# Filler matmuls in a two-layer transformer block: lower levels of estimated TensorE occupancy

## The chip, the cores and the metric

The kernel runs on one core of a Trainium2 chip. A core has five engines with queues of their own: TensorE (PE, matrix products into the PSUM memory), VectorE (DVE), ScalarE (ACT), GpSimd (POOL) and SyncE (SP, which here issues DMAs). They meet through semaphores only. The metric is the time of one execution in microseconds (us), as the device measures it. A change counts by the median of several runs. Beside the runs there is one profiled execution, from which all rows of the profile come.

## The reference

Two layers, each an attention block and a gated feed-forward block (FFN), both with a residual sum and a layer norm without weights. The same weights serve both layers.

```python
def _A_ref(x, wqkv, wo):              # x: 1 x 2048 x 512, 32 heads of 16
    qkv = (x @ wqkv).reshape(B, S, 3, H, Dh)   # then q, k, v by head
    scores = einsum("bhqd,bhkd->bhqk", q, k) * Dh ** -0.5
    p = softmax(scores)
    o = einsum("bhqk,bhkd->bhqd", p, v)
    return o.reshape(B, S, D) @ wo
def _B_ref(x, w_gate, w_up, w_down):  # 512 -> 1792 -> 512
    return (gelu(x @ w_gate) * (x @ w_up)) @ w_down

x = A_x
x = x + _A_ref(layernorm(x), wqkv, wo)
x = x + _B_ref(layernorm(x), w_gate, w_up, w_down)
...   # both lines once more
```

Inputs are bfloat16. A head has only 16 dimensions, so a score matmul fills few rows of the array, while every one of the 2048 x 2048 scores of 32 heads must be read out of PSUM.

## The kernel before

**The two passes over the scores.** The softmax needs the largest score of each row of queries. The kernel computes the scores twice. Pass 1 (line 1165, matmuls `PS<-KT,QT`) puts queries on partitions: a tile is 128 queries by 512 keys of one head, and DVE takes the maximum along the keys (line 1180). Usually two tiles lie in neighbouring banks of PSUM and one DVE instruction of 1024 columns takes both (a pair); where only one bank is free, one instruction takes one tile (a single). The maxima of a unit (four heads, up to 512 queries) are collected in PM, reduced and transposed on DVE (lines 684, 686) and moved by SP into a spare row of the queries QT (line 701). The keys KT hold ones in that row, so pass 2 (line 1062, `PS<-QT,KT`, keys on partitions) yields scores with the maximum already taken off. ACT takes the exponential of one or two tiles (line 1039) into SCR, and PE multiplies these by the values VP (line 1085), with a column of ones that sums the weights. A unit's sums are read by ACT (line 714) and divided on POOL (lines 720, 725). In a few places two tiles of pass 1 are folded: ACT writes the positive part of a difference (line 1019) and DVE adds and reduces in one custom instruction with a read of its result (line 1175).

Both passes use 32 rows of the array per matmul, and up to four such matmuls, on different rows, run at once. PSUM has eight banks: pass 1 has banks 0 to 3, pass 2 mostly 3 to 6, and bank 7 holds the sums of the values.

**Everything else** goes in between as chains of small steps: layer norm and transposes (line 576), projections of Q, K and V, the output projection and the FFN (all matmuls of line 494). Their results are read out by DVE or ACT, whichever the rule `pick` names by how far pass 1 leads pass 2. The second layer takes its queries in blocks of 512, 512, 512, 256 and 256; the first in four of 512. At the end DVE has no more reductions to do, ACT finishes the exponentials, and the last output projection and FFN follow.

**The planner.** The order of all instructions is made when the kernel is built. A loop (the `while True` behind `warm_emit`) keeps an estimated clock for each engine, `clk`. At each step it knows the estimated time `now` on PE and a list `act` of PE work, each with its columns at 1/2400 us, at a quarter for a matmul of 32 rows. From them it has the estimated occupancy of PE over the last 3.413 us:

```python
            load = sum(c for _, _, c in act) / 3.413
```

The loop then records the next piece of PE work with the instruction that reads its result: a pair or single of pass 1, a tile or two of pass 2, both, a piece of a chain, or a filler. A filler (`warm_emit`, line 1198) multiplies a zero matrix ZER with 240 columns of the value weights WV into a part of a bank that nobody reads, so it changes no result. It is a matmul of 128 rows and 240 columns.

The occupancy enters in two places. The slack that may be spent to record both passes together is 0.1 us where it is under the level WARM, else 0.15 us (line 1283):

```python
                if G <= min(max(S1, T1), max(S2, T2)) + (SPC if load < WARM else SPLIT):
```

And fillers (`want` is WARM, `must` is WARML; BOOST is 0):

```python
            cool = load < want and now > 12 and warm_bank(now) is not None
            if G is not None and now >= G - 0.02 and not (cool and load < must):
                ...
            if cool and (G is None or now + 0.12 <= lim or load < must):
                warm_emit(warm_bank(now))
```

Under the upper level a filler is recorded where the planner sees a hole of 0.12 us ahead of the next pair. Under the lower level it is recorded even where a pair is due. Since the order is fixed when the kernel is built, a filler that is recorded is executed wherever it stands. On the chip each engine works through its own list and waits on semaphores where it must.

## Time and profile before

| | |
|---|---|
| time, median of 3 runs (lowest to highest) | 2621.01 us (2617.53 to 2625.14) |
| the profiled execution: time, span | 2617.2 us, 2615.4 us |
| mean granted clock of TensorE | 0.999 |
| matmuls on PE, fillers among them | 30171, 2715 |
| maxima on DVE (line 1180): pairs, singles | 1464, 1024 |
| exponentials on ACT (line 1039): pairs, singles | 1550, 996 |

How to read it: the page gives busy time of each engine, and in it PE means matmuls and PEld the loading of weights, which overlaps them. A matmul's record reaches to the modelled end of its pipeline, so PE that is shown busy is not at its peak. Groups are by line, engine, operation and shape, with count, busy time, mean ns of one, and the idle time of the engine just before them with what ended it. The chain is followed back from the last instruction. A view of stretches gives busy time for each engine in each stretch and the clock that was granted to TensorE there, where 1.00 is full speed.

### The profile page before, as it was taken

To read this page: it belongs to the slowest core of one execution; us is meant where nothing else is said; L and a number is where in the kernel's file an instruction comes from. 1 tells how busy PE (TensorE), PEld (TensorE's weight loads), DVE (VectorE), ACT (ScalarE), POOL (GpSimd) and SP (SyncE) were. 2 spreads that over 40 slices of the span, in tenths; PEclk is the share of its full clock that TensorE was granted. 3 is DMA by queue.
4 is the path that set the end of the run, shared out by engine and by line. 5 is a ranking of instruction groups with operands and counts; after the bars stand their busy time and mean duration, and the time that the engine had idled before them with its cause. 6 is when DMAs were issued, how large, how long until landed. Compare 5 with 4: busy or idle time off the path is not lost.

```text
span 2615.4 us, 67983 instructions
## 1 busy us (share of the span) xinstructions
PE 2504.4 (96%) x30171; PEld 1186.5 (45%) x30171; DVE 2480.6 (95%) x2965; ACT 2341.4 (90%) x3172; POOL 540.8 (21%) x521
## 2 busy tenths in 40 slices
PE   7999999999999999999999999999999999999998
PEld 2444443444434444344423555544444445444555
DVE  7999999999999999999999999999999999999991
ACT  8799998999989998999952999979998899989996
POOL 3011022221222212222132111111112311232201
PEclk9999999999999999999999999999999999999999
DMA  3110000000000000000000000000000000000000
GB/s 101 34 56 8 4 4 2 4 4 4 4 3 3 4 4 3 8 4 12 9 8 9 2 4 4 4 4 6 8 6 4 6 6 3 4 4 11 4 6 5
DMA packets 27125, 25.03 MB, mean 10 GB/s; under 512 B 9168, under 2 KB 25808, under 8 KB 26832
## 3 DMA queue, kind: packets, MB, share of 16 engines
q1 hardware_dynamic: 26832, 20.69, 2.8%
q8 instruction: 236, 3.87, 0.6%
q14 instruction: 57, 0.47, 0.1%
HBM read 9.70 MB, written 2.10 MB: 5 GB/s over the span
## 4 chain that ended last, share of the span: by engine, by line
PE 51%; DVE 30%; ACT 18%; issue 1%; POOL 0%; POOLq 0%; ACTq 0%
DVE PM L1180 28%; ACT SCR L1039 16%; PE PS L1165 16%; PE PS L494 12%; PE PS L1085 11%; PE PS L1062 6%; PE PS L1198 5%; DVE SCR L1175 1%; PE PS L576 1%; PE PS L1012 0%; ACT AO L738 0%; DVE ST L521 0%; ACT SCR L1019 0%; ACT L1039 0%; DVE HT L820 0%
## 5 line engine op out<-in xcount | busy, mean ns | idle before, releaser
L1180 DVE TENSOR_REDUCE PM<-PS 128x2 f32<-128x1024 f32 (+1 forms) x2488 | 2327.9, 997 | 59.2 <-PE PS L1062 30.2
L1039 ACT ACTIVATE SCR<-PS 128x1024 bf16<-128x1024 f32 (+1 forms) x2546 | 2037.6, 878 | 87.4 <-PE PS L1062 44.1
L1062 PE MATMUL PS<-QT,KT 32*128 32x512 bf16 (+1 forms) x4608 | 988.0, 360 | 32.8 <-ACT SCR L1039 29.3
L1165 PE MATMUL PS<-KT,QT 32*128 32x512 bf16 x4024 | 974.0, 385 | 38.5 <-DVE PM L1180 21.9
L1085 PE MATMUL PS<-VP,SCR 128*128 128x51 bf16 (+1 forms) x16384 | 804.5, 188 | 6.3 <-ACT SCR L1039 3.7
L1085 PEld LDWEIGHTS PS<-VP,SCR 128*128 128x128 bf16 x16384 | 566.5, 96 | 491.0 <-issue 445.3
L1165 PEld LDWEIGHTS PS<-KT,QT 32*128 32x128 bf16 x4024 | 234.3, 91 | 517.2 <-DVE PM L1180 300.6
L1198 PE MATMUL PS<-WV,ZER 128*128 128x240 bf16 x2715 | 457.9, 266 | 5.6 <-ACT SCR L1039 4.9
L720 POOL TENSOR_TENSOR RL<-ACCS,CM 128x16 f32<-128x16 f32 (+1 forms) x64 | 175.9, 2749 | 1296.5 <-ACT ACCS L714 1296.5
L1062 PEld LDWEIGHTS PS<-QT,KT 32*128 32x128 bf16 x4608 | 244.1, 91 | 142.3 <-ACT SCR L1039 114.6
L1198 PEld LDWEIGHTS PS<-WV,ZER 128*128 128x128 bf16 x2715 | 207.5, 96 | 69.3 <-issue 49.7
L828 POOL TENSOR_TENSOR HT<-HT,AO 128x512 bf16<-128x512 bf16 (+1 forms) x105 | 111.5, 1062 | 312.7 <-ACT AO L826 312.6
L810 ACT ACTIVATE HT<-PS 128x512 bf16<-128x512 f32 (+1 forms) x126 | 69.0, 549 | 78.9 <-PE PS L494 78.0
L494 PE MATMUL PS<-WD,HT 128*128 128x512 bf16 x448 | 131.0, 382 | 1.5 <-POOL HT L828 1.4
L494 PE MATMUL PS<-XNT,WU 128*128 128x512 bf16 (+1 forms) x504 | 129.4, 358 | 1.7 <-DVE PM L1180 0.6
L494 PE MATMUL PS<-XNT,WG 128*128 128x512 bf16 (+1 forms) x504 | 121.4, 361 | 0.0
L740 POOL TENSOR_TENSOR X<-X,AO 128x512 f32<-128x512 f32 x43 | 54.4, 1267 | 216.2 <-ACT AO L738 216.2
L865 POOL TENSOR_TENSOR KD<-KT 128x512 bf16<-128x512 bf16 x71 | 81.7, 1152 | 47.1 <-PE PS L1012 47.1
L826 ACT ACTIVATE AO<-PS 128x512 f32<-128x512 f32 (+1 forms) x105 | 59.2, 564 | 12.0 <-PE PS L494 10.8
L494 PEld LDWEIGHTS PS<-XNT,WG 128*128 128x128 bf16 x504 | 38.9, 98 | 47.6 <-issue 28.5
L725 POOL TENSOR_TENSOR ATT<-ACCS,RL 128x256 bf16<-128x256 f32 (+1 forms) x72 | 41.1, 571 | 90.3 <-DVE RL L718 85.3
L494 PEld LDWEIGHTS PS<-XNT,WU 128*128 128x128 bf16 x504 | 34.0, 97 | 34.8 <-issue 22.4
(78 smaller groups left out, 801.0 us busy)
## 6 DMA issues: line engine op xcount, KB each, us to landing
KT<-SG SPq DMA_DIRECT2D x64, 64.0 KB
QT<-SG SPq DMA_DIRECT2D x56, 64.0 KB
QT<-MT SPq DMA_DIRECT2D x224, 1.0 KB
out_dram<-AO SPq DMA_DIRECT2D x16, 128.0 KB, 1.7
WG<-in_B_w_gate_dram SPq DMA_DIRECT2D x4, 448.0 KB, 5.1
WU<-in_B_w_up_dram SPq DMA_DIRECT2D x4, 448.0 KB, 3.9
WD<-in_B_w_down_dram SPq DMA_DIRECT2D x4, 384.0 KB, 4.5
SCR<-in_A_x_dram SPq DMA_DIRECT2D x2, 512.0 KB, 5.2
```

The costliest lines, as they stand in the source:

```text
L494: ins = e.matmul(out_ap, lhsT=l, rhs=r_, start=(i == 0), stop=(i == n - 1))
L720: emit("pool", lambda e: e.tensor_tensor(RL[:, s, 0:4 * nq], lsum, CM1[:, 0:4 * nq], op=ALU.pow), r=[("ACCS", s), ("CM1",)], w=[("RL", s)] ...
L810: emit("act", lambda e, bg=bg, ft=ft: e.activation(HT[:, ft, 0:n], bank(bg)[:, 0:n], ACTF.Gelu_apprx_tanh), r=[BK[bg]], w=[("HT", ft)], du ...
L826: emit("act", lambda e, bu=bu, o=o: e.activation(AO[:, o, 0:n], bank(bu)[:, 0:n], ACTF.Copy), r=[BK[bu]], w=[("AO", o)], dur=0.055 + n / 1 ...
L828: emit("pool", lambda e, ft=ft, o=o: e.tensor_tensor(HT[:, ft, 0:n], HT[:, ft, 0:n], AO[:, o, 0:n], op=ALU.mult), r=[("AO", o), ("HT", ft) ...
L865: emit("pool", lambda e: e.tensor_tensor(KD[:, s, :], KT[:, g, ka * 512:(ka + 1) * 512], KT[:, g, kb * 512:(kb + 1) * 512], op=ALU.subtrac ...
L1039: emit("act", lambda e: e.activation(dst, src, ACTF.Exp, scale=DH ** -0.5), r=[BK[bk + i] for i in range(cnt)], w=[("PT", i) for i in slot ...
L1062: ins = e.matmul(bank(bk)[:, i * n:(i + 1) * n], lhsT=KT[32 * j:32 * j + 32, g, kt * 128:(kt + 1) * 128], rhs=QT[32 * j:32 * j + 32, s, 0: ...
L1085: ins = e.matmul(acc, lhsT=PT[:, slot, i * n + qt * 128:i * n + (qt + 1) * 128], rhs=AP(VP, (kt * H + 4 * g + j) * 17, [[NTT * H * 17, 128 ...
L1165: ins = e.matmul(bank(b), lhsT=QT[32 * j:32 * j + 32, s, qt * 128:(qt + 1) * 128], rhs=KT[32 * j:32 * j + 32, g, kb * 512:(kb + 1) * 512], ...
L1180: emit("dve", lambda e: e.tensor_reduce(po, PS[:, bs[0]:bs[0] + cnt, :], axis=AX.X, op=ALU.max), r=bks, w=[("PM", sm) + h[1:] for h in hs] ...
L1198: return e.matmul(PS[:, b, NACC:512], lhsT=ZER[:, :], rhs=WV[:, 0, 0:512 - NACC], start=(b != 7), stop=(b != 7), skip_group_check=True)
```

## The change

Two default values of `_build` change: the upper level of estimated occupancy, WARM, from 0.55 to 0.46, and the lower one, WARML, from 0.42 to 0.34. Since the planner decides every step by what came before, the recorded order changes from the first few microseconds on, on every engine. The computation is the same.

```diff
 def _build(nc, x_in, wqkv, wo, wg, wu, wd, out, layer_blocks=((512, 512, 512, 512), (512, 512, 512, 256, 256)),
-           ..., PVC=47, WARM=0.55, WARML=0.42, NPV=10, BOOST=0.0, ...):
+           ..., PVC=47, WARM=0.46, WARML=0.34, NPV=10, BOOST=0.0, ...):
```

More of the change, by code (lines that the diff above doesn't have):

```diff
@@ L174, in _build @@
 def _build(nc, x_in, wqkv, wo, wg, wu, wd, out, layer_blocks=((512, 512, 512, 512), (512, 512, 512, 256, 256)),
-           n_ahead=6, n_pre=6, S1C=0.45, S2C=0.42, OV=0.3, PD=70, FDUE=20, LIM=-0.05, NT=1, AHD=2.0, DUEM=-4, FDL2=-8, OPD=-6, ft_tok=512, n_pt=8, n_qt=8, SPLIT=0.15, SPC=0.1, PVC=47, WARM=0.55, WARML=0.42, NPV=10, BOOST=0.0, LAG=62, LAGT=75, GP=2, SING=0, DUE=0, END=360, LAGE=10, FD=280, FDL=-10, QD=32, KD_=24, VD=20, FL=8, FMAX=6, NKD=2, FLOOK=2, FX=0.1):
+           n_ahead=6, n_pre=6, S1C=0.45, S2C=0.42, OV=0.3, PD=70, FDUE=20, LIM=-0.05, NT=1, AHD=2.0, DUEM=-4, FDL2=-8, OPD=-6, ft_tok=512, n_pt=8, n_qt=8, SPLIT=0.15, SPC=0.1, PVC=47, WARM=0.46, WARML=0.34, NPV=10, BOOST=0.0, LAG=62, LAGT=75, GP=2, SING=0, DUE=0, END=360, LAGE=10, FD=280, FDL=-10, QD=32, KD_=24, VD=20, FL=8, FMAX=6, NKD=2, FLOOK=2, FX=0.1):
     S = x_in.shape[1]
```

## The prediction

> **What bounds the kernel now.** I read the page first: the busy line, then the chain that ended last, then the fillers' own group.

> ```profile
> PE 2504.4 (96%) x30171; PEld 1186.5 (45%) x30171; DVE 2480.6 (95%) x2965; ACT 2341.4 (90%) x3172; POOL 540.8 (21%) x521
> ...
> PE 51%; DVE 30%; ACT 18%; issue 1%; POOL 0%; POOLq 0%; ACTq 0%
> ...
> L1198 PE MATMUL PS<-WV,ZER 128*128 128x240 bf16 x2715 | 457.9, 266 | 5.6 <-ACT SCR L1039 4.9
> ```

> Three engines are over 90% busy. PE's 96% says least, because matmuls overlap in the record and 2715 of PE's 30171 instructions are fillers. So I looked at each stage (stretch, its length, then busy time of PE, PEld, DVE, ACT, POOL, the granted clock of TensorE, and DMA):

> ```profile
> 75.00:700.00 625.00, 593.99 (x7523) 287.59 (x7523) 615.50 (x686) 591.29 (x816) 116.67 (x105) 1.00 0.04 12
> 700.00:1300.00 600.00, 581.06 (x6920) 266.00 (x6917) 590.38 (x669) 555.83 (x790) 136.75 (x117) 1.00 0.02 5
> 1300.00:1450.00 150.00, 145.60 (x836) 49.16 (x833) 140.68 (x211) 70.87 (x104) 43.79 (x53) 1.00 0.03 8
> 1450.00:2000.00 550.00, 532.64 (x7008) 263.82 (x7007) 538.05 (x659) 520.93 (x626) 79.43 (x56) 1.00 0.02 5
> 2000.00:2550.00 550.00, 535.86 (x6926) 260.76 (x6926) 527.01 (x640) 507.55 (x681) 129.91 (x125) 1.00 0.02 5
> 2550.00:2616.00 66.00, 55.54 (x648) 35.76 (x646) 11.54 (x25) 40.24 (x62) 9.91 (x16) 0.97 0.02 5
> ```

> DVE is the bound of layer 0: idle only 9.5 us of 625 and 9.6 of 600. In layer 1 DVE idles 12 and 23 us of 550, and in several 25 us slices there (1475 to 1500, 1575 to 1600, 1875 to 1900) ACT is busy for all 25.00 us, so the two take turns. From 75 to 2550 us DVE idles 63 us in all. That is the whole prize a freer PE can win in these stretches. Of it, DVE waits for PE (total us, times, longest):

> ```profile
> DVE PM L1180 <- PE PS L1062: 30.2, 113, 0.7
> DVE PM L1180 <- PE PS L1165: 10.3, 43, 0.6
> DVE SCR L1175 <- PE PS L1165: 2.1, 8, 0.7
> ```

> 42.6 us. (L1062 stands there because score matmuls of both passes sit in one group on PE.) Going through DVE's waits on matmuls one by one in the trace, 89 of them, 16.1 us, have a filler as PE's last work before the group that DVE waited for.

> The clock matters as much. Four windows of 3.41 us, a thin one in the middle of layer 1 and three at the end:

> ```profile
> 1559.17:1562.59 3.42, 2.89 (x43) 1.41 (x39) 3.03 (x6) 3.42 (x5) 1.41 (x1) 1.00 0.00 0
> 2583.17:2586.58 3.41, 3.17 (x26) 2.33 (x24) 1.90 (x4) 0.60 (x1) 1.27 (x1) 1.00 0.00 0
> 2586.58:2590.00 3.42, 0.40 (x4) 0.23 (x4) 0.42 (x2) 0.13 (x1) 2.59 (x5) 1.00 0.00 0
> 2590.00:2593.41 3.41, 3.22 (x18) 2.50 (x19) 0.42 (x1) 2.13 (x3) 0.13 (x1) 0.50 0.00 0
> ```

> After the window in which PE was busy 0.40 us, the granted clock is 0.50 for one window and then whole again. It is the only drop after the start. I cut the trace at that phase into windows and weighed streamed columns as the kernel's estimate does (a 32-row matmul at a quarter). Over 716 windows from 88 to 2532 us the weighted share is 0.554 in the mean, 0.388 at least (the thin window shown), and 0.063 in the window ahead of the drop. All this trace says of the level that drops the clock is that it lies between 0.063 and 0.388.

> **The change part by part.** Prices are busy time over count from these rows, since successive instructions overlap a little: DVE pair 1734.2/1464 = 1.185 us, DVE single 690.5/1024 = 0.674, ACT pair 1536.5/1550 = 0.991, ACT single 599.7/996 = 0.602.

> ```profile
> L1180 DVE TENSOR_REDUCE PM<-PS 128x2 f32<-128x1024 f32 x1464 | 1734.2, 1218 | 48.0 <-PE PS L1062 26.3 <-PE PS L1165 14.0
> L1039 ACT ACTIVATE SCR<-PS 128x1024 bf16<-128x1024 f32 x1550 | 1536.5, 1054 | 74.7 <-PE PS L1062 37.7 <-PE PS L1165 9.6
> ...
> L1180 DVE TENSOR_REDUCE PM<-PS 128x1 f32<-128x512 f32 x1024 | 690.5, 682 | 11.3 <-PE PS L1062 3.8 <-PE PS L1165 2.5 <-PE PS L1012 0.5
> L1039 ACT ACTIVATE SCR<-PS 128x512 bf16<-128x512 f32 x996 | 599.7, 603 | 12.7 <-PE PS L1062 6.4
> ```

> The planner's lists of both programs can be counted without running them.

> *Fillers.* 1552 in place of 2715, 1163 fewer. Fillers in a run start 0.103 us apart (a run of four takes 0.57 us, a single one 0.26), so PE is given back 1163 x 0.103 = 120 us. Most of it lay in holes while PE waited for a bank and is worth nothing; the cover is DVE's own queue. What counts is the part ahead of due work. Counted where they are recorded, 167 fillers of before displaced a pair that was due (estimate below the lower level); 63 do in the changed program: 104 x 0.103 = 10.7 us. The other way: 43% of the 16.1 us of DVE waits right behind a filler is 6.9 us. Bounds: nothing, if DVE then waits for its bank or for its own queue; 43% of all 63 us of DVE's idle time = 27 us. I take 9, between the two counts.

> *Split tiles.* The same estimate picks between two slacks for pairing the passes (line 1283), and everything behind is reordered. Layer 0 on DVE: 7 pairs fewer, 18 singles more, 4 folded tiles (0.725 us with its read) fewer: -8.3 + 12.1 - 2.9 = +0.9 us, in full on the path. Layer 1 on DVE: -10 pairs, +28 singles, -2 folded: -11.9 + 18.9 - 1.5 = +5.5, and one projection copy and one gated product move from ACT to DVE, +1.4. Layer 1 on ACT: +17 pairs, -33 singles: 16.8 - 19.9 = -3.0; three fewer fold activations (1.02 each) and the two moved ones give -4.3 more over both layers. DVE and ACT take turns there, so of +6.9 and about -4 I take +2, with -4 and +7 as ends.

> *The end.* After the last reduction 100 score matmuls of 256 columns remain in place of 108, two ACT pairs less where ACT is the bound (2550 to 2579): -2.0 us, between 0 and -2. Then come output projection and FFN, which wait for POOL with or without fillers.

> *SP and POOL.* The same 527 instructions on SP, a few in another order; POOL has four fewer. Their queues sit idle most of the time: no cost, unless a move of K or Q lands behind its first use (then up to a few us, inside the ends above).

> Sum: -9 + 0.9 + 2 - 2 = -8 us. The profiled execution took 2617.2 us (span 2615.4 and 1.8 around it), 3.8 under the median of 2621.0. So 2609 on its scale, **2613 us** beside the median, -0.3%. About 0.3% (8 us) is what a measurement of this kernel can tell from no change, so this sits on the edge of it.

> [...] In the trace the clock fell only after a window with 0.40 us of PE work, and in none of the 716 windows between, the thinnest at 0.388. [...]

> **The rivals.**
> *The clock drops in attention (slower).* Fillers fall from 0.102 of a window to 0.058 in the mean, and the floor that the planner defends by 0.08. Shifted by 0.044, 11 of the 716 windows come under the lowest share seen safe (0.388); shifted by 0.08, 67 do. At half clock a filler took 408 ns against 265. In attention PE is busy for 95% of the time, so a cold window does little over half its work: between nothing lost and 1.7 us, I take 1.2. With 20 such windows, +24 us: 2637. With all 67, +80. It decides from 7 windows (8 us) on. For it: the windows that the change thins are just those under the level of 0.42. Against it: at 0.388 there is no sign of it, and the level can be anywhere down to 0.063.
> *The relief is off the path (slower or no change).* DVE is back to back in layer 0, so the 9 us turn into waits for a bank, and layer 1 pays DVE's extra singles in full: +0.9 + 6.9 = +8, less 0 to 2 at the end: about 2628. For it: the stages' rows, DVE 98% busy; against it: 42.6 us of waits on PE.
> *PE was the real bound.* Fillers are 5% of the chain, and 43% of all DVE idle time goes: -27 + 1 = about 2595. Against it: 62% of DVE's waits on PE (26.5 of 42.6 us) begin behind projections or the second pass, not behind a filler.
> That the change does nothing is excluded by the 1163 missing fillers.

> **How the numbers follow.** Forecast (-8, own range 2604 to 2620): 0.41, half of it beyond -0.3%. Clock drops: 0.34, nearly all slower. Relief off the path: 0.17, half slower, half within. PE the real bound: 0.08. Faster 0.20 + 0.08, and a little for a dip smaller than feared: 0.30. Slower 0.31 + 0.09 = 0.40. Same 0.30. The range runs from 2599, which leaves half of the last rival out, to 2648, which leaves out drops in more than about 30 windows (0.12).

> **What would show it.** The fillers' group at 1552; DVE busy near 2488 and ACT near 2334; DVE's waits on PE down from 42.6 to about 34; the granted clock at 1.00 in every stage but the last. The prediction is wrong if the clock row shows 0.9 or less in attention slices, if DVE's idle time does not fall, or if waits on ACT take its place.

## The result, and the profile after

The changed kernel took 2691.78 us (median of four runs, 2676.91 to 2704.43) beside 2621.55 (four runs of the kernel before): a ratio of 1.0266, with a 95% interval of 1.0208 to 1.0324. It is slower by 70 us. Four more runs of it, in a later group of runs, gave 1.0301 (1.0287 to 1.0316). I had forecast 2613 us and given 0.34 to the case that the clock drops.

The profiled execution took 2686.8 us. The page of the changed kernel, busy line, the granted clock in 40 slices and the chain:

```profile
PE 2508.1 (93%) x28820; PEld 1157.0 (43%) x29008; DVE 2488.6 (93%) x2984; ACT 2340.8 (87%) x3149; POOL 540.1 (20%) x517
...
PEclk9787899997999989989899899999999999999999
...
PE 43%; DVE 30%; ACT 24%; issue 1%; POOL 1%; POOLq 0%; ACTq 0%
```

The fillers' group in the view of groups by shape says that the change did what it says: 1552 fillers.

```profile
L1198 PE MATMUL PS<-WV,ZER 128*128 128x240 bf16 x1552 | 296.2, 284 | 2.1 <-ACT SCR L1039 1.7 <-ACT SCR L1019 0.3
```

DVE is busy for 2488.6 us and ACT for 2340.8, near the 2488 and 2334 that I had counted: the same work at nearly the same price. DVE's busy time is only 8 us above before (2480.6), and the rest of the 70 us is idle time of DVE. The stages (stretch, length, busy time of PE, PEld, DVE, ACT, POOL, granted clock, DMA) tell with what it came:

```profile
75.00:700.00 625.00, 583.84 (x6690) 267.56 (x6720) 586.36 (x654) 552.46 (x757) 106.90 (x95) 0.88 0.04 12
700.00:1300.00 600.00, 561.34 (x6468) 251.47 (x6530) 577.80 (x662) 547.30 (x779) 141.98 (x121) 0.96 0.02 5
1300.00:1450.00 150.00, 144.01 (x1079) 51.76 (x1087) 139.93 (x181) 98.64 (x142) 40.33 (x47) 0.95 0.02 5
1450.00:2000.00 550.00, 517.32 (x6228) 245.58 (x6258) 530.12 (x667) 478.69 (x564) 74.46 (x56) 0.97 0.02 5
2000.00:2550.00 550.00, 523.58 (x6527) 251.46 (x6570) 524.86 (x644) 506.33 (x673) 136.91 (x124) 0.99 0.02 5
2550.00:2686.00 136.00, 119.36 (x1549) 66.68 (x1552) 75.51 (x107) 103.84 (x139) 15.11 (x25) 0.95 0.02 5
```

In the first stage DVE idles 38.6 us of 625 where it idled 9.5 before, and the clock there is 0.88 in place of 1.00. DVE's waits on PE between 75 and 2550 us (total, times, longest) have grown:

```profile
DVE PM L1180 <- PE PS L1062: 72.7, 176, 2.0
DVE PM L1180 <- PE PS L1165: 21.5, 75, 1.3
DVE SCR L1175 <- PE PS L1165: 2.7, 9, 1.0
```

That is 96.9 us in place of 42.6, and the longest is 2.0 us in place of 0.7. The drops themselves, in windows of 3.41 us of the changed kernel (same columns): a thin window, four cold ones behind it (cold means a granted clock of 0.50, warm one of 1.00), and the first warm one.

```profile
69.06:72.47 3.41, 2.40 (x14) 0.80 (x13) 3.08 (x5) 0.60 (x1) 0.00 (x0) 1.00 0.29 73
72.47:75.89 3.42, 3.42 (x15) 1.20 (x14) 2.66 (x5) 0.00 (x0) 0.00 (x0) 0.50 0.01 4
75.89:79.30 3.41, 3.41 (x18) 1.41 (x18) 3.34 (x9) 0.70 (x1) 0.00 (x0) 0.50 0.00 0
79.30:82.71 3.41, 3.37 (x17) 1.19 (x16) 3.00 (x7) 1.34 (x2) 1.19 (x2) 0.50 0.01 1
82.71:86.13 3.42, 3.42 (x26) 1.51 (x24) 2.70 (x3) 1.02 (x1) 0.00 (x0) 0.50 0.02 5
86.13:89.54 3.41, 3.03 (x35) 1.43 (x34) 3.32 (x10) 2.40 (x3) 0.00 (x0) 1.00 0.00 0
```

PE was busy for 2.40 of 3.41 us in the window that cost the clock; no idle window was needed. And the clock did not come back after one window. In this execution there are 19 drops and 78 cold windows, 4.1 to a drop. The longest spell has 18; here it is, and beside it the same 61.44 us of before:

```profile
232.90:294.34 61.44, 60.95 (x540) 25.69 (x539) 46.72 (x48) 44.81 (x60) 8.23 (x7) 0.50 0.02 4
```

```profile
232.90:294.34 61.44, 58.21 (x781) 29.73 (x779) 60.98 (x62) 59.43 (x80) 4.93 (x7) 1.00 0.01 2
```

At half clock PE is the bound: busy for 60.95 us of 61.44, while DVE does 46.72 us of work in place of 60.98. Of DVE's 12.7 us of idle time ahead of its pairs in this stretch, 12.4 end with a score matmul. That is 14.3 us lost in 18 windows, 0.79 us each.

### The profile page after: what moved, and what is told of

The parts are those of the page before. It is cut to its first block, busy times and chain, and to the rows that moved or that the text cites. A ratio compares the mean times of both kernels' runs of the same rounds, so it can differ in the third digit from the quotient of the medians.

```text
span 2685.0 us, 65461 instructions
## 1 busy us (share of the span) xinstructions
PE 2508.1 (93%) x28820; PEld 1157.0 (43%) x29008; DVE 2488.6 (93%) x2984; ACT 2340.8 (87%) x3149; POOL 540.1 (20%) x517
## 4 chain that ended last, share of the span: by engine, by line
PE 43%; DVE 30%; ACT 24%; issue 1%; POOL 1%; POOLq 0%; ACTq 0%
DVE PM L1180 29%; ACT SCR L1039 22%; PE PS L1165 14%; PE PS L494 11%; PE PS L1085 9%; PE PS L1062 5%; PE PS L1198 4%; PE PS L576 1%; ACT AO L738 0%; ACT SCR L1019 0%; DVE SCR L1175 0%; ACT ATTT L511 0%; ACT AO L826 0%; ACT ACCS L714 0%; PE PS L1012 0%
## 5 line engine op out<-in xcount | busy, mean ns | idle before, releaser
L1180 DVE TENSOR_REDUCE PM<-PS 128x2 f32<-128x1024 f32 (+1 forms) x2517 | 2338.0, 989 | 117.1 <-PE PS L1062 74.8
L1039 ACT ACTIVATE SCR<-PS 128x1024 bf16<-128x1024 f32 (+1 forms) x2528 | 2041.1, 879 | 149.4 <-PE PS L1062 120.8
L1165 PE MATMUL PS<-KT,QT 32*128 32x512 bf16 x4030 | 1019.6, 401 | 64.9 <-DVE PM L1180 44.3
L1062 PE MATMUL PS<-QT,KT 32*128 32x512 bf16 (+1 forms) x4608 | 1022.4, 375 | 45.6 <-ACT SCR L1039 40.6
L1085 PE MATMUL PS<-VP,SCR 128*128 128x51 bf16 (+1 forms) x16384 | 832.0, 190 | 17.5 <-ACT SCR L1039 11.9
L1085 PEld LDWEIGHTS PS<-VP,SCR 128*128 128x128 bf16 x16384 | 585.1, 98 | 550.9 <-issue 470.3
L1165 PEld LDWEIGHTS PS<-KT,QT 32*128 32x128 bf16 x4030 | 237.0, 91 | 528.9 <-DVE PM L1180 316.4
L1062 PEld LDWEIGHTS PS<-QT,KT 32*128 32x128 bf16 x4608 | 242.6, 92 | 187.7 <-ACT SCR L1039 154.3
L1198 PE MATMUL PS<-WV,ZER 128*128 128x240 bf16 x1552 | 296.2, 284 | 2.1 <-ACT SCR L1039 1.7
L1198 PEld LDWEIGHTS PS<-WV,ZER 128*128 128x128 bf16 x1552 | 127.4, 101 | 52.7 <-issue 41.9
L494 PE MATMUL PS<-WD,HT 128*128 128x512 bf16 x390 | 121.3, 389 | 7.4 <-issue 4.1
L494 PE MATMUL PS<-XNT,WU 128*128 128x512 bf16 (+1 forms) x449 | 117.2, 354 | 6.3 <-issue 4.4
L511 ACT ACTIVATE XNT<-PS 128x512 bf16<-128x512 bf16 x57 | 34.1, 612 | 20.5 <-PE PS L576 20.1
```

Of the source, the lines that this page charges most:

```text
L494: ins = e.matmul(out_ap, lhsT=l, rhs=r_, start=(i == 0), stop=(i == n - 1))
L1039: emit("act", lambda e: e.activation(dst, src, ACTF.Exp, scale=DH ** -0.5), r=[BK[bk + i] for i in range(cnt)], w=[("PT", i) for i in slot ...
L1062: ins = e.matmul(bank(bk)[:, i * n:(i + 1) * n], lhsT=KT[32 * j:32 * j + 32, g, kt * 128:(kt + 1) * 128], rhs=QT[32 * j:32 * j + 32, s, 0: ...
L1085: ins = e.matmul(acc, lhsT=PT[:, slot, i * n + qt * 128:i * n + (qt + 1) * 128], rhs=AP(VP, (kt * H + 4 * g + j) * 17, [[NTT * H * 17, 128 ...
L1165: ins = e.matmul(bank(b), lhsT=QT[32 * j:32 * j + 32, s, qt * 128:(qt + 1) * 128], rhs=KT[32 * j:32 * j + 32, g, kb * 512:(kb + 1) * 512], ...
L1180: emit("dve", lambda e: e.tensor_reduce(po, PS[:, bs[0]:bs[0] + cnt, :], axis=AX.X, op=ALU.max), r=bks, w=[("PM", sm) + h[1:] for h in hs] ...
```

## The experiments

Behind each time stand its ratio to runs of the kernel before from the same group of runs and, in brackets, the 95% interval. Two theories stood against each other. *Clock*: a window whose share of streamed columns, weighted by rows, is too low costs the clock, and the 70 us are the cold windows. *Order*: the plan is a new one on every engine, and the new order costs part or all of it.

**Fillers thinned in the order of before.** Three of seven planned fillers are left out when the program is written, so 1552 are executed, and every engine's order is that of before. (Fillers change no result.)

```diff
-        def emit_pe(fn, n, cols, r=(), w=(), rows=None, used=None):
-            sch.op("pe", fn, r=r, w=w)
+        def emit_pe(fn, n, cols, r=(), w=(), rows=None, used=None, live=True):
+            live and sch.op("pe", fn, r=r, w=w)
...
-            emit_pe(fn, 1, 512 - NACC, r=[("ZER",), ("WV",)], w=[BK[b]])
+            emit_pe(..., live=(lambda k: k * 3 // 7 == (k - 1) * 3 // 7)(next(nf)))
```

> The order of before, with three of every seven fillers (1163 of 2715) recorded in the estimate but not executed. Clock theory (the clock falls after a window whose weighted share is under about 0.375 and stays down about four windows, 0.9 us lost in each): taking three sevenths of the measured fillers out of the windows of before leaves 17 of them under 0.375, so about 17 drops, 17 x 4.1 x 0.9 = 63 us: about 2680 us, granted clock near 0.955. Order theory (the new order of the work costs the 70 us): the order is that of before and PE has less to do, so 2600 to 2622 us, whatever the clock shows.

Measured: 2632.6 us, 1.0062 (1.004 to 1.0085), clock 0.968 to 0.977, 35 cold windows in the profile. Slower though PE has less to do and the order is the same, so the clock costs time; but 16 us, not 63. I read this as half a victory for the order theory. It was none: at the 0.90 us that a cold window costs (worked out below) 35 of them are 32 us, and the thinned program also gained what the missing fillers had cost. From 101 to 1395 us its clock held. There the same 1472 instructions of DVE, from the same one on, took this long before (first line) and in the thinned program:

```profile
98.12:1402.82 1304.70, 1256.70 (x14654) 571.59 (x14653) 1278.62 (x1472) 1177.70 (x1657) 291.26 (x267) 1.00 0.03 9
101.10:1394.63 1293.53, 1220.70 (x14091) 534.58 (x14091) 1273.04 (x1472) 1173.76 (x1657) 291.62 (x267) 1.00 0.03 9
```

That is 11.2 us less with 563 fillers fewer (58 us of PE time at 0.103 us each). Half of it, 5.6 us, is idle time of DVE, the other half is busy time.

**Fillers doubled in the order of the changed kernel.** Each is executed twice.

```diff
-                return e.matmul(PS[:, b, NACC:512], ...)
+                return [e.matmul(PS[:, b, NACC:512], ...) for _ in range(2)][-1]
```

> The order of the changed kernel, each of its 1552 fillers executed twice in a row. Clock theory: the thin windows gain about as much share as they lost, so at most a few drops, clock 0.99 or more, 2610 to 2635 us (the second copies are 160 us of PE time, most of it in holes). Order theory: 2680 us or more, since the order is that of the changed kernel and PE has more to do.

Measured: 2724.02 us, 1.0414 (1.0397 to 1.0432), at a clock of 0.991 to 0.996. Both the time and the clock went up, which the clock theory had not allowed. DVE's largest waits of this version, 75 to 2550 us:

```profile
DVE PM L1180 <- PE PS L1062: 77.2, 228, 1.8
DVE PM L1180 <- PE PS L1165: 28.2, 102, 1.5
```

105 us of waits on PE at nearly full clock. Gone through one by one in the trace, about 50 us of DVE's waits begin right behind a filler, against about 14 in the version with fillers in holes (below): many second copies stood ahead of due work. The experiment changed two things at once and tells the theories apart only together with a later one.

**One level put back at a time.**

```diff
-WARM=0.46, WARML=0.34
+WARM=0.46, WARML=0.42     (first)
+WARM=0.55, WARML=0.34     (second)
```

> Levels 0.46 and 0.42: only the lower level is put back. The plan has 2143 fillers, but 1342 of them ahead of a due pair (before 167). Clock theory: by the kernel's own estimate 1.3% of the time is under 0.375 (3.1% in the changed kernel, 0.3% before): about 9 drops, +33 us, and the displaced pairs on top: 2640 to 2670 us. If the lower level alone guarded the clock: 2610 to 2625 us. Order theory says nothing on the clock; with yet another order, 2640 or more.

> Levels 0.55 and 0.34: only the upper level is put back. 2550 fillers, 38 ahead of a due pair. Clock theory: 0.7% of the time under 0.375, about 5 drops, +18 us: 2630 to 2645 us, clock near 0.99. If the lower level alone guarded the clock, as many drops as in the changed kernel: 2670 us or more. Order theory: near 2680 us.

Measured: 2672.13 us (1.0197, 1.0168 to 1.0226) at clocks of 0.987 to 0.996, and 2652.06 us (1.0132, 1.0106 to 1.0158) at 0.979 to 0.988. Neither level alone is enough. Both times lie a little above what the clock theory had given (2640 to 2670 and 2630 to 2645 us). With the upper level low and the lower one high, the clock nearly holds but 1342 fillers stand ahead of due pairs. With the upper one high, the time lies between before and changed, as the clock does.

**Extra fillers where the estimate is under 0.40**, in the order of the changed kernel, not counted by the plan.

```diff
...   # warm_emit(b, 0) records a filler that the plan's clock does not count
+        def guard_clock(now, load):
+            while (mode[0] == "full" and now > 12 and warm_bank(now) is not None
+                   and load + 0.1 * sum(t > now - 3.413 for t in ext) / 3.413 < 0.40):
+                warm_emit(warm_bank(now), 0)
+                ext.append(now)
...
+            guard_clock(now, load)
```

> The order of the changed kernel. Where the kernel's estimate, extra fillers included, falls under 0.40 and PE's last work used the whole array, extra fillers are put in that the plan does not count: 604 of them, 62 us of PE time, some of it ahead of due work. Clock theory: nearly all drops gone, clock 0.99, and the time comes back to 2615 to 2635 us. Clock and order theory (the thinned order of before lost only 16 us for 35 cold windows, 0.45 us each, so of the 70 us about half are the clock's and half come with the new order): clock 0.99, and still about 2645 to 2660 us.

Measured: 2657.76 us, 1.0164 (1.0126 to 1.0202), clocks of 0.982 to 0.996. As the mixed theory had it. Yet its single runs showed something better than its median: 2676.4 us at 0.982, 2657.5 at 0.992, 2658.0 at 0.993, 2652.0 at 0.996. One program, one order, and the time follows the clock by 1.7 us for each 0.001.

**The pairing slack alone.** The level WARM also chooses between two slacks (line 1283). Both ways:

```diff
+(SPC if load < 0.55 else SPLIT)   (in the changed kernel)
+(SPC if load < 0.46 else SPLIT)   (in the kernel before)
```

> The changed levels for fillers, but the slack for recording both passes together still switches at 0.55. 1567 fillers. If the pairing rule makes the new order dear: 2640 to 2665 us at a clock near 0.95. If it is the fillers' places in the plan: 2680 to 2700 us.

> The levels of before for fillers, but the slack for recording both passes together switches at 0.46. 2736 fillers. If the pairing rule is dear by itself: 2635 to 2660 us at a clock of 0.99 or more. If not: 2612 to 2625 us.

Measured: 2728.41 us (1.0439, 1.0409 to 1.0469) at clocks of 0.919 to 0.929, and 2628.39 us (1.0038, 1.0023 to 1.0053) at 0.995 to 0.999. The first missed both expectations: with the old pairing rule there are even more cold windows (112 in its profile). The second says that the rule, with the order that follows from it, is worth some 7 us where the clock holds (its run at 0.999 took 2624.2 us).

**Lean fillers in the order of before.** A planned filler is executed only where the estimate, less those left out, is under a level: 0.46 (1732 executed), then 0.50 (2150).

```diff
...   # emit_pe takes `live` as in the thinned version
+            live = load - 0.1 * sum(t > now - 3.413 for t in ghost) / 3.413 < 0.46
+            live or ghost.append(now)
-            emit_pe(fn, 1, 512 - NACC, r=[("ZER",), ("WV",)], w=[BK[b]])
+            emit_pe(fn, 1, 512 - NACC, r=[("ZER",), ("WV",)], w=[BK[b]], live=live)
```

> The order of before; a planned filler is executed only where the estimate without the fillers left out is under 0.46: 1732 of 2715 are executed, those in the thin stretches among them. All theories: the clock holds (0.99 or more, at most three drops in attention). If fillers cost DVE time, as I forecast (up to 9 us): 2606 to 2615 us, faster than before. If they lie in holes: 2615 to 2622 us, the same as before. More than 2630 us would mean that leaving fillers out costs something else than the clock.

> The order of before; a planned filler is executed only where the estimate without those left out is under 0.50: 2150 of 2715 are executed. The runs of one program differ in how many windows fall cold, and the time falls with the clock by 1.4 to 1.9 us per 0.001 of mean granted clock, which is about one us per cold window. Clock theory: at most two drops in attention, clock 0.99 to 0.999, and at full clock 2610 to 2614 us (the run of the version at 0.46 that had a clock of 0.997 took 2611.6). If fillers are free wherever they are planned: 2616 to 2622 us.

Measured at 0.46: 2630.72 us, 1.0047 (1.0007 to 1.0088), with runs from 2611.6 us at a clock of 0.997 to 2643.0 at 0.977. All theories had expected a clock of 0.99 or more here, and four of five runs missed it; in the profile one drop at 561 us stayed for 26 windows. At 0.50: 2618.4 us, 1.0000 (0.9991 to 1.0009), ten runs at 0.994 to 0.996 and one at 0.999 that took 2612.1 us. So there is a gain in leaving fillers out, and two drops in attention (six cold windows in the profile) eat it.

**The changed kernel again**, for more runs of the same program.

> The changed kernel again, for more runs of one and the same program. Clock theory: the new runs lie on the line of the first four, about 1.43 us per 0.001 of granted clock (2686.8 at 0.950, 2704.4 at 0.936), which meets the clock of before at about 2615 us. Order theory: times between 2675 and 2705 us without regard to the clock.

Measured: 2693.35, 2702.75, 2696.37, 2695.43 us at clocks of 0.945, 0.938, 0.943, 0.942. All eight runs lie on a line with a correlation of -0.99: 1.42 us (standard error 0.08) for each 0.001 of clock, and 2615.8 us (4.4) at the 0.999 of before. A cold window lowers the mean clock of such a run by 3.413 x 0.5 / 2690 = 0.00063, so it costs 0.90 us. The lines of the other programs with four runs or more at a clock of 0.96 and up are mostly steeper, from 1.4 to 1.9 us, so 0.90 is the price in this kernel and not a constant.

**No fillers at all.** Both levels are 0.

> Both levels at 0: no fillers at all. By the kernel's own estimate 31% of the time is under 0.375, so the clock theory expects the clock to be down for most of the attention stages: granted clock 0.55 to 0.75, and at 1.4 to 1.9 us per 0.001 some 2900 to 3200 us. If only idle windows threw the clock, it would stay at 0.99 or more and the time at 2600 to 2620 us.

Measured: 2906.67 us, 1.1102 (1.108 to 1.1125), at a clock of 0.703 to 0.707. Its granted clock on the page:

```profile
PEclk9555557975589756997697555579656975579796
```

PE has 2715 matmuls fewer to run than before and the kernel is 289 us slower. The time fits the clock theory's range (2900 to 3200 us) at its low end.

**Fillers in the plan's holes only**, in the order of the changed kernel. This one was made for the question that was left: the line above is extended from a clock of 0.955, and the guarded version lay above it.

```diff
...   # warm_emit(b, 0) as in the version with extra fillers under 0.40
+            k = now
+            while k + 0.12 <= tn and now > 12 and warm_bank(now) is not None and load + 0.1 * sum(t > now - 3.413 for t in ext) / 3.413 < 0.55:
+                warm_emit(warm_bank(now), 0)
+                ext.append(k)
+                k += 0.12
             clk["pe"] = max(now + 0.01, tn)
```

> The order of the changed kernel, with 972 extra fillers that the plan does not count, put only where the plan leaves PE a hole of at least 0.12 us, as long as the estimate with them is under 0.55: 2524 fillers in all. If the whole loss is the clock's (the eight runs of the changed kernel lie on 2615.8 us + 1.42 us for each 0.001 that the clock is under 0.999): the time falls to that line's value at the new clock, plus at most 11 us for the extra fillers (planned fillers cost 11% of their 0.103 us where 561 of them were left out); at a clock of 0.99, 2629 to 2640 us. If half of the loss is the order's: 2655 us or more at a clock of 0.99, as with the 604 extra fillers put ahead of due work.

Measured: 2628.05 us, 1.004 (1.0024 to 1.0056), ten runs; 2622.17 us at a clock of 0.999, 2639.0 at 0.990. Its stages 75 to 700 and 700 to 1300 us read like those of before:

```profile
75.00:700.00 625.00, 595.11 (x7411) 283.90 (x7410) 615.43 (x690) 581.51 (x806) 113.56 (x100) 0.99 0.04 12
700.00:1300.00 600.00, 576.19 (x6869) 261.05 (x6867) 589.03 (x668) 556.63 (x789) 139.89 (x121) 1.00 0.02 5
```

DVE, ACT, POOL and SP have the order of the changed kernel to the instruction, PE has 972 fillers more, and all but 10 of the 70 us are gone (2617.76 us is before in the same group of runs), all but about 5 at full clock. The order theory falls as an account of the 70 us. DVE's waits of this version, 75 to 2550 us, are back near those of before:

```profile
DVE PM L1180 <- PE PS L1062: 27.6, 105, 0.9
DVE PM L1180 <- PE PS L1165: 16.9, 65, 1.0
```

What made the doubled and the guarded versions dear fits with where their extra fillers stood: at full clock, by their own lines, they lie at about 2716 and 2647 us, 101 and 31 us above the changed kernel's 2616, for 160 and 62 us of added PE time. Those fillers, part of them ahead of due work, cost half their PE time or more in the mean. In the plan's holes 972 of them (100 us) cost about 7, from a line whose end has a standard error of 4.4.

**A version that beats both.** The order of before; in stretches where traces of the thinned versions had a rolling window under 0.40, all planned fillers are executed (81 stretches, 1437 of 4024 tiles of pass 1), elsewhere those under 0.46.

```diff
-            live = load - 0.1 * sum(t > now - 3.413 for t in ghost) / 3.413 < 0.46
+            live = any(x <= nt[0] <= y for x, y in THIN) or load - 0.1 * sum(t > now - 3.413 for t in ghost) / 3.413 < 0.46
```

> The order of before. In the stretches (1437 of 4024 tiles of pass 1) where traces of the thinned versions showed a rolling window under 0.40, all planned fillers are executed; elsewhere only where the estimate without those left out is under 0.46: 2154 of 2715 in all, as many as at 0.50, but at other places. Clock theory: no drop in attention, clock 0.998 or more, and 2609 to 2613 us, the relief that 561 fillers fewer give (the run of the version at 0.50 with a clock of 0.999 took 2612.1). If fillers are free where they are planned: 2617 to 2619 us.

Measured: 2611.36 us (2610.84 to 2611.98) beside 2617.61: 0.9972 (0.9961 to 0.9983), every run at a clock of 0.999. As many fillers as at level 0.50, but where they are needed. Its groups of reductions on DVE by shape, pairs and singles:

```profile
L1180 DVE TENSOR_REDUCE PM<-PS 128x2 f32<-128x1024 f32 x1464 | 1731.5, 1216 | 46.1 <-PE PS L1062 25.3 <-PE PS L1165 13.9
L1180 DVE TENSOR_REDUCE PM<-PS 128x1 f32<-128x512 f32 x1024 | 689.5, 681 | 12.0 <-PE PS L1062 3.8 <-PE PS L1165 2.5 <-PE PS L1012 0.5
```

Idle time before the two groups is 58.1 us in place of 59.3, so idle time ahead of the reductions shows only 1.2 of the 6.3 us.

Not tried: fillers of 32 rows, which would have separated weighting by rows from streamed time directly.

## Why the prediction was wrong, point by point

- **The bound and the work.** Right. DVE and ACT have the busy time that was counted from the plan. In the version with fillers in holes they are 2485.5 and 2334.8 us, against the 2488 and 2334 that I had counted. At full clock the order of the changed kernel is near before, 2616 us by the line of its own runs and 2622 with fillers in its holes, against my 2613.
- **Relief on PE, -9 us.** The size was in the right range, and the mechanism is half confirmed. At a held clock, 563 fillers fewer gave 11.2 us in half of the thinned execution, 5.6 of them idle time of DVE, which is what I had counted. In the version that beats both, 561 fewer gave 6.3 us, but only 1.2 of it is idle time ahead of the reductions, while DVE's busy time is 4.8 us less (2475.8 in place of 2480.6). I had counted waits alone. Why DVE's busy time falls is open: a pair is 2 ns shorter there (1216 in place of 1218 ns), but pairs differ as much between programs whatever their fillers (1215 ns with 1552 in the thinned version, 1218 with 1567 where the old pairing slack was put back, 1217 with 3104 in the doubled one).
- **The likeliest case, that the clock holds.** This is the step that failed: the sum held the clock at 1.00 in every attention stage, at no cost, and the runs show 0.88 to 0.99 there and 70 us. I had bounded the dropping level between 0.063 and 0.388 and let the wide interval speak for a level far down. It lies just under the upper end. I cut the 15 profiled executions into windows on the grid of their own drops and weighed streamed columns as in the prediction, from each matmul's recorded start. A warm window under 0.36 was followed by a drop in 97 of 103 cases, between 0.36 and 0.37 in 25 of 47, between 0.37 and 0.39 in 11 of 127, from 0.39 up in none of 10432.
- **The rival's price, "a cold window does little over half its work ... I take 1.2".** Per window it is 0.90 us by the runs and 0.79 in the longest spell, both inside my 0 to 1.7. DVE did 77% of its work there, not a little over half: I had read PE's recorded busy time as work that half a clock would halve. The number of drops was near too, 20 taken and 19 in the profile, but by luck: 20 was picked between counts of 11 and 67, for a level of 0.388.
- **The step that was missing: a drop is not one window.** I took its length from the single drop that the trace before had, at 2590 us, where the FFN's matmuls at full width followed at once and filled the cold window to 0.95 (columns weighted by rows and counted at half speed: neighbouring fillers start 0.200 us apart at a clock of 0.50 and 0.102 at 1.00, medians in the changed kernel's trace). In attention most cold windows are filled to 0.55 to 0.75 (61 of all 78 in the changed kernel's profile), and the clock stays down. Why no fuller was not taken apart: PE shows as busy nearly throughout (60.95 of 61.44 us in the longest spell). In the 15 executions, of 722 cold windows under a share of 0.70, 15 released the clock, of 133 between 0.70 and 0.75, 28, and of 94 from 0.75 up, 90. The doubled version agrees: its seven cold spells are filled to 0.72 to 0.90, and each is over after one window. So 24 us became 78 windows x 0.90 = 70 us, the measured loss, and the range ended 44 us too low. (The 0.90 comes from the same kernel's runs; that the loss is the clock's is shown apart from it, by the version with fillers in holes.)
- **How idle the window was.** The one drop that I had to go by stood behind a window with 0.40 us of PE work. In the changed kernel's profile only the last of the 19 drops has such a window ahead of it (0.52 us busy); ahead of the other 18 PE was busy for 1.62 to 3.41 of 3.41 us. And if only idle windows cost the clock, the version without fillers would have kept 0.99 or more; it ran at 0.703 to 0.707.
- **What would have shown it.** I had named "0.9 or less in attention slices": the page of the changed kernel has slices of 7 and 8. DVE's waits on PE, which I had put at 34 us, went up to 96.9.

## What to carry to other kernels

In this kernel the clock was a cliff beside a slope: leaving out fillers gained a tenth to a fifth of their PE time, and one window too thin cost some four windows at 0.9 us. Where a kernel keeps its clock with fillers, count streamed columns weighted by rows in windows of 3.41 us, look for the share below which its own clock drops (in these profiles 11 of 127 warm windows between 0.37 and 0.39 lost it, and none of 10432 from 0.39 up), and put fillers into holes of the plan, where 100 us of them cost about 7 here. When runs of one program differ, lay their times against their clocks before any story about the order: the line through the changed kernel's own runs had the answer that three altered versions blurred.
